# A new placement of the first 40 rounds of an attention and SoLU feed-forward kernel: DMA queues, rounds and engines of the weight pieces, loads of later batches, products with v, and the first steady pair

## The chip, the core and the metric

The kernel runs on one core of a Trainium2 chip. The core has five engines that run side by side, each in its own order: TensorE (PE; its weight loads are listed apart as PEld), VectorE (DVE), ScalarE (ACT), GpSimd (POOL) and SyncE (SP), which only issues DMA transfers here. ScalarE can issue DMAs too, and then the issue stands in ScalarE's own order of work. The metric is the device time of one execution in microseconds (us).

## The reference: thresholded attention, then a feed-forward layer with SoLU

All data are float32, except that the two weight matrices arrive as float64.

```python
# attention: q, k, v of shape (8, 8, 576, 64), tau = 0.02
scores = (1/8) * q @ k^T
scores = where(scores >= max(scores) - tau, scores, -1e9)
attn   = exp(scores - max) / (sum + 1e-9)
x      = (attn @ v), heads put side by side: (4608, 512)
# feed-forward: w_in (512, 1024), w_out (1024, 512), g_ln (1024)
h    = x @ w_in
solu = h * softmax(h)
ln   = (solu - mean) / sqrt(var + 1e-6) * g_ln
out  = ln @ w_out
```

## The kernel before

**Rounds.** The attention is cut into 144 rounds ("slots"), 18 for each of the 8 batches. A round takes 128 query rows of a pair of heads (or the left-over rows of four heads) against all 576 keys. Its steps are: scores on PE (`scores`, L492); the row's threshold on VectorE (`maxes`, L514); ramp and exponential on ScalarE (`ramp` L529, `exps` L538); one round later the sums' reciprocal and the scaling on GpSimd (`normalise`, L545 to L548) and the transposes of 32x32 blocks on VectorE (`blocks`, L559), which fill a tile T. After every second round DMAs on SP's queue move T into wT with its quarters of rows in place (`spread`, L580, L582, L589). Some rounds later PE multiplies wT with v (`attend_steps`, L619), and ScalarE copies the product to xh or xe (`attended`, L652).

**Feed-forward.** A group of 128 tokens gets h on PE (L1041 before round 30; L735 for pairs of groups and L759 for single groups after), then a chain of maximum, exponential, product, sums, mean and variance, and normalisation (L1056 to L1130), a transpose through DMAs (V, L1144) and VectorE (uT, L1157), the product with w_out on PE (L1175), a copy `ob` (L1195) and the store (L1216). Groups that are done before round 30 are called fronts; their steps stand in the table `HO` and `CHAIN`. From round `START` = 30 on, `steady_round` runs the same work in a fixed pattern: `new_pair` treats two groups together with the steps of `PAIR0` (first pairs), `PAIR` or `PAIRZ`, and `new_one` a single group by `ONE0`, `ONE` or `ONEZ`. In these tables a step has a place in a round (0 to 3: begin, early, middle, late) and a number of rounds after the group's start.

**Weights.** The weights are float64 and are turned into float32 by integer arithmetic in 16 pieces of 128x512 (pieces 0 to 7 of w_in, 8 to 15 of w_out). A piece has up to six jobs: `weight_load` (DMA into one of four raw buffers, chosen by `RAW`; the queue is ScalarE's where `QUEUE` is 1, else SP's), `weight_a` (one scaling `em` by the engine that `UNIT` names: 0 VectorE and 2 GpSimd at L286, 1 ScalarE at L282; the sign on VectorE, L291; the low half on ScalarE, L294), `weight_b` (VectorE, L306), `weight_c` (GpSimd, L316), `weight_gain` (the gain g_ln, by `GAIN`: 0 ScalarE L322, 1 VectorE and 2 GpSimd L324) and `weight_d` (copies of two halves to other rows, by `MOVER`: 0 ScalarE L337, 1 VectorE L339, 2 GpSimd L343, 3 DMA L347). `PIECE` gives the quarter of a round of each job (round = number // 4), `MOVE` that of the copies. Before round 0, pieces 0 to 2 are loaded. A raw buffer that is used again is loaded only when all three reads of `weight_a` of the piece before are done.

**Loads.** The q, k and v of batch 0 are loaded at the start and, for the later half of v, at the rounds in `FETCH`; batch 1's by `FETCH` as well. From batch 2 on q and k arrive as they lie in memory (`load_natural`) and are turned by VectorE ("flip", L209) and DMAs (L211). `LOAD2`, `TURN2`, `ENDS2` and `V2` say in which round batch 2's loads, turns, end rows and parts of v stand. `PREP` says in which rounds the k and q of batch 1 are turned on PE (L360) in the free part of the scores' PSUM tiles, and `EASED` whether ScalarE alone copies them out or shares this with VectorE (L396 to L439).

**Order.** Everything is recorded in the order of the program text, round by round, and each engine runs its instructions in that order. [...] `LAG` changes in which round after `LAG_PV` = 3 a product with v falls due, `SPLIT` how many of its matmuls run in the first of two rounds, and `SEVEN` when GpSimd forms sums of blocks of w_in (L692), which the pairs use.

```python
            jobs_of = zip(
                (2, 3, 1, 0, 4, 5),
                (weight_load, weight_a, weight_b, weight_c, weight_gain, copies),
                (*PIECE[x], MOVE.get(x, PIECE[x][4])),
            )
...
            pv_due.append((s + LAG_PV + LAG.get(s, 0), (b, kind, hp)))
```

Of the kernel before, what the change touches and what calls it, by code (L numbers as in the profile page):

```python
# [1582 lines left out]
```

## Time and profile before

| | |
|---|---|
| median of 3 runs | 845.41 us (841.01 to 851.94) |
| the profiled execution | 846.98 us |
| its span, first to last instruction | 845.0 us |
| granted TensorE clock, mean | 0.981 |
| PE busy | 799.7 us, 95% |
| VectorE, ScalarE, GpSimd busy | 671.5, 604.4, 565.2 us |
| DMA traffic | 167.44 MB, mean 198 GB/s |

A profile records one execution. A row of a group tells line, engine, operation, tile written <- tiles read, shape and count, then the busy time, the mean duration in ns, and the engine's idle time just before these instructions with what ended it. Slices are 1/40 of the span; a digit is the busy share in tenths. A row with "q" behind the engine's name (SPq, ACTq) belongs to its sequencer: an issue or a wait. The DMA share is the mean busy share of 16 DMA engines.

### The profile page before, as it was taken

To read this page: it belongs to the slowest core of one execution; us is meant where nothing else is said; L and a number is where in the kernel's file an instruction comes from. 1 tells how busy PE (TensorE), PEld (TensorE's weight loads), DVE (VectorE), ACT (ScalarE), POOL (GpSimd) and SP (SyncE) were. 2 spreads that over 40 slices of the span, in tenths; PEclk is the share of its full clock that TensorE was granted. 3 is DMA by queue.
4 is the path that set the end of the run, shared out by engine and by line. 5 is a ranking of instruction groups with operands and counts; after the bars stand their busy time and mean duration, and the time that the engine had idled before them with its cause. 6 is when DMAs were issued, how large, how long until landed. Compare 5 with 4: busy or idle time off the path is not lost.

```text
span 845.0 us, 36864 instructions
## 1 busy us (share of the span) xinstructions
PE 799.7 (95%) x15345; PEld 589.3 (70%) x15345; DVE 671.5 (79%) x1324; ACT 604.4 (72%) x1214; POOL 565.2 (67%) x1031
## 2 busy tenths in 40 slices
PE   4769899999899999999999999999999999999997
PEld 3435567767566886777776677767786677788786
DVE  3888968867889878888889888888888888787362
ACT  5979977676777777778787777878787687876231
POOL 3976867866757758585867758585867758574330
PEclk9679999999999999999999999999999999999999
DMA  7999688887877868887788768887788767555122
GB/s 231 272 231 259 181 221 225 213 220 191 222 224 208 228 149 240 229 216 207 204 244 223 204 163 246 225 221 196 216 238 218 207 159 211 144 152 137 37 62 52
DMA packets 100535, 167.44 MB, mean 198 GB/s; under 512 B 18248, under 2 KB 47952, under 8 KB 100368
## 3 DMA queue, kind: packets, MB, share of 16 engines
q1 hardware_dynamic: 99040, 162.82, 72.3%
q8 instruction: 121, 1.98, 1.0%
q10 hardware_dynamic: 1328, 2.26, 0.9%
q14 instruction: 46, 0.38, 0.1%
HBM read 46.14 MB, written 9.44 MB: 66 GB/s over the span
## 4 chain that ended last, share of the span: by engine, by line
PE 75%; ACT 7%; DMA 5%; POOL 4%; DVE 4%; issue 3%; SPq 2%; DVEq 0%; ACTq 0%; POOLq 0%
PE ov L1175 19%; PE h L735 16%; PE s_ps L492 14%; PE ov L619 12%; PE o_ps L1175 6%; PE h L759 4%; DMA wT<-T 3%; ACT w L529 2%; ACT w L538 2%; PE h_ps L1041 2%; DVE w L514 2%; PE pv L619 2%; POOL w L548 1%; DMA raw<-in_moe_w_out_dram 1%; DMA q<-in_q_dram 1%
## 5 line engine op out<-in xcount | busy, mean ns | idle before, releaser
L529 ACT ACTIVATE w<-s_ps,nth 128x576 f32<-128x576 f32 x282 | 199.6, 741 | 128.5 <-DVE nth L514 113.8
L514 DVE CUSTOM_DVE_ANT_0 w<-s_ps,tau_t 128x576 f32<-128x576 f32 x282 | 201.0, 749 | 55.0 <-PE s_ps L492 36.8
L548 POOL TENSOR_SCALAR w<-w,sm 128x576 f32<-128x576 f32 x288 | 219.0, 772 | 14.3
L559 DVE STREAM_TRANSPOSE T<-w 128x576 f32<-128x576 f32 x288 | 207.7, 756 | 17.8 <-POOL w L548 13.8
L538 ACT ACTIVATE w<-w,ntau 128x576 f32<-128x576 f32 x288 | 219.7, 768 | 0.0
L1175 PE MATMUL ov<-w,uT 64*64 64x256 f32 x3456 | 208.0, 376 | 0.7 <-issue 0.7
L492 PE MATMUL s_ps<-kT,qT 64*64 64x64 f32 (+1 forms) x2048 | 175.4, 424 | 15.1 <-ACT w L529 12.5
L619 PEld LDWEIGHTS ov<-wT,v 64*64 64x64 f32 x4752 | 150.6, 133 | 46.9 <-issue 33.6
L1175 PEld LDWEIGHTS ov<-w,uT 64*64 64x64 f32 x3456 | 160.6, 133 | 26.2 <-issue 1.2
L619 PE MATMUL ov<-wT,v 64*64 64x128 f32 (+1 forms) x4752 | 153.6, 259 | 1.2 <-DMA wT<-T 0.7
L545 POOL TENSOR_SCALAR sm<-sm 128x2 f32<-128x2 f32 x144 | 35.1, 244 | 143.5 <-ACT w L538 138.2
L546 POOL TENSOR_TENSOR sm<-sm,mone 128x2 f32<-128x2 f32 x144 | 104.1, 723 | 12.0
L735 PE MATMUL h<-w,xh 64*64 64x512 f32 x832 | 104.7, 591 | 0.6 <-POOL mark L110 0.4
L492 PEld LDWEIGHTS s_ps<-kT,qT 64*64 64x64 f32 x2048 | 71.4, 139 | 42.3 <-ACT w L529 19.1
L1175 PE MATMUL o_ps<-w,uT 64*64 64x256 f32 x1088 | 66.4, 377 | 0.7 <-ACT xh L652 0.5
L735 PEld LDWEIGHTS h<-w,xh 64*64 64x64 f32 x832 | 43.9, 133 | 31.4 <-issue 20.4
L1175 PEld LDWEIGHTS o_ps<-w,uT 64*64 64x64 f32 x1088 | 57.5, 133 | 10.8 <-issue 4.0
L1130 DVE TENSOR_SCALAR u<-u,rs,nb 128x1024 f32<-128x1024 f32 x32 | 28.8, 900 | 43.4 <-ACT V L1124 43.3
L1157 DVE STREAM_TRANSPOSE uT<-V 128x1024 f32<-128x1024 f32 x36 | 44.3, 1229 | 17.1 <-PE ov L1175 6.9
L538 ACT ACTIVATION_READ_ACCUMULATOR w<-w,ntau 128x1 f32 x288 | 55.7, 193 | 0.0
L735 PE MATMUL h<-k,sum 64*64 64x512 f32 x312 | 51.8, 589 | 0.0
L1124 ACT ACTIVATE V<-u,nb,rs 128x1024 f32<-128x1024 f32 x36 | 44.6, 1238 | 6.5 <-POOL nb L1102 6.4
(132 smaller groups left out, 1015.9 us busy)
## 6 DMA issues: line engine op xcount, KB each, us to landing
wT<-T SPq DMA_DIRECT2D x132, 288.0 KB, 4.5
wT<-T SPq DMA_DIRECT2D x256, 144.0 KB, 3.9
out_dram<-ob SPq DMA_DIRECT2D x71, 128.0 KB, 2.5
V<-u SPq DMA_DIRECT2D x136, 64.0 KB, 2.3
wT<-T SPq DMA_DIRECT2D x14, 576.0 KB, 6.4
q<-in_q_dram SPq DMA_DIRECT2D x24, 288.0 KB, 3.8
q<-in_k_dram SPq DMA_DIRECT2D x24, 288.0 KB, 4.3
v<-in_v_dram SPq DMA_DIRECT2D x12, 576.0 KB, 5.3
```

The lines of the kernel that those rows point to most:

```text
L492: nc.tensor.matmul(out=ps[h][ROWS[y], ks], lhsT=lhsT, rhs=d["kT"][ROWS[h], ks], start=True, stop=True,)
L514: nc.vector.tensor_tensor_reduce(out=w, in0=ps[:, 0:S], in1=(zero if loose else tau_t).to_broadcast([P, S]), scale=1.0, scalar=BIG, op0=AL ...
L529: nc.scalar.activation(out=d["w"][x], in_=d["w"][x] if d["loose"] else d["ps"][x][:, 0:S], func=AF.Prelu, bias=d["nth"][x], scale=-1.0, al ...
L538: nc.scalar.activation(out=w, in_=w, func=AF.Exp, bias=ntau, scale=1.0, accum_out=sm[:, x : x + 1])
L546: nc.gpsimd.tensor_tensor(out=sm, in0=sm, in1=mone, op=ALU.pow)
L548: nc.gpsimd.tensor_scalar(out=w, in0=w, scalar1=sm[:, x : x + 1], scalar2=1.0, op0=ALU.mult, op1=ALU.mult)
L559: nc.vector.transpose(out=T[:, :, r, :, h, :], in_=w.rearrange("p (c m x) -> p c m x", c=2, x=32))
L619: nc.tensor.matmul(out=to, lhsT=d["v"][ROWS[u], (h0 + h - u) % 4 if b > 1 else h0 + h, m ^ 4 * u if m < 8 and b < 2 else m,], rhs=rhs, sta ...
L735: mm = nc.tensor.matmul(out=h[ROWS[y], 512 * bank : 512 * bank + 512], lhsT=x[ROWS[r], ROWS[y]], rhs=w[ROWS[r]], start=c == 0 and (n, r, k ...
L1124: nc.scalar.activation(out=V, in_=u, func=AF.Identity, bias=nb, scale=rs)
L1157: nc.vector.transpose(out=uT, in_=d["V"].rearrange("p y (m x) -> p m y x", x=32))
L1175: nc.tensor.matmul(out=to[ROWS[z], 0:256], lhsT=d["uT"][ROWS[r], m].rearrange("p y x -> p (y x)"), rhs=w2[ROWS[r], m ^ r, 256 * z : 256 * ...
```

## The change

Only tables change, with no change to the arithmetic. Pieces 3 to 6 are issued from ScalarE's queue, and the quarters of rounds of the jobs of nearly all pieces are set anew. Scalings, gains and copies go to other engines. Loads, turns and parts of v of batches 1 and 2 get other rounds, the lags of three products with v become smaller, the splits move by a few matmuls, and the tables of the first single groups and the first pair get new places. In a table such as `CHAIN` the order of entries matters too where two steps fall on the same place.

```diff
     PAIR0 = {
+        "sum_b": (3, 8),
         "sums_a": (3, 0),
         "keep_a0": (3, 0),
-        "add_a0": (1, 1),
+        "norm_a": (3, 8),
         "sums_b": (2, 1),
+        "keep_b1": (3, 3),
+        "add_a1": (0, 5),
+        "max_a": (0, 5),
+        "add_b1": (0, 5),
+        "add_a0": (3, 0),
+        "exp_a": (1, 5),
         "keep_a1": (2, 3),
-        "keep_b1": (3, 3),
-        "add_a1": (3, 4),
-        "add_b1": (0, 5),
-        "max_a": (1, 5),
-        "exp_a": (1, 5),
+        "turn_a": (1, 10),
         "mul_a": (3, 6),
-        "sum_a": (0, 7),
+        "norm_b": (0, 12),
...
-        "stats_b": (0, 10),
+        "turn_b": (2, 14),
+        "stats_b": (3, 9),
+        "sum_a": (0, 7),
         "scale_b": (1, 11),
-        "norm2_b": (3, 12),
+        "norm2_b": (1, 13),
     }
     ONE0 = {
         "max": (0, 3),
+        "mul": (3, 3),
         "exp": (0, 3),
-        "mul": (1, 3),
-        "stats": (2, 4),
-        "sum": (1, 5),
+        "turn": (3, 9),
+        "stats": (3, 4),
         "scale": (3, 6),
-        "norm": (0, 7),
-        "norm2": (1, 7),
-        "turn": (3, 9),
+        "norm2": (0, 8),
+        "sum": (1, 4),
+        "norm": (3, 6),
     }
-    SPLIT = {30: 0, 32: 30, 34: 6, 36: 5, 38: 16, 40: 30, 42: 7, 44: 23, 46: 11, 56: 27, 74: 21, 92: 23, 110: 26, 128: 14}
-    SEVEN = {0: 21, 1: 21, 2: 24, 3: 25, 5: 25, 4: 26, 7: 26, 6: 29}
-    PIECE = {0: (-1, 1, 3, 6, 7, ), 1: (-1, 3, 5, 10, 11, ), 2: (-1, 8, 11, 14, 15, ), 3: (3, 12, 15, 18, 19, ), 4: (3, 15, 18, 21, 25, ), 5: (7, 20, 23, 26, 27, ), 6: (11, 23, 25, 30, 31, ), 7: (13, 27, 31, 34, 35, ), 8: (23, 31, 35, 38, 39, ), 9: (23, 35, 39, 42, 43, ), 10: (29, 39, 43, 46, 47, ), 11: (35, 43, 47, 50, 51, ), 12: (39, 49, 51, 54, 55, ), 13: (43, 52, 55, 58, 59, ), 14: (43, 55, 59, 62, 63, ), 15: (55, 59, 63, 66, 67, )}
+    SPLIT = {30: 0, 32: 32, 34: 0, 36: 4, 38: 14, 40: 34, 42: 8, 44: 20, 46: 12, 56: 26, 74: 20, 92: 25, 110: 29, 128: 10}
+    SEVEN = {0: 17, 1: 21, 2: 25, 3: 25, 5: 26, 4: 26, 7: 25, 6: 28}
+    PIECE = {0: (-1, 0, 3, 6, 7), 1: (-1, 3, 5, 10, 11), 2: (-1, 8, 11, 14, 15), 3: (7, 12, 15, 18, 19), 4: (3, 15, 17, 21, 25), 5: (7, 18, 23, 26, 27), 6: (11, 23, 25, 30, 31), 7: (18, 27, 31, 34, 35), 8: (19, 31, 35, 38, 38), 9: (22, 35, 39, 42, 43), 10: (27, 39, 42, 46, 47), 11: (35, 44, 46, 50, 51), 12: (39, 47, 51, 55, 55), 13: (43, 52, 55, 58, 59), 14: (43, 55, 59, 62, 64), 15: (55, 59, 63, 66, 67)}
-    QUEUE = {0: 1, 1: 1, 2: 1, 3: 0, 4: 0, 5: 0, 6: 0, 7: 0, ...}
-    UNIT = {0: 0, 1: 2, 2: 2, 3: 2, 4: 1, 5: 2, 6: 1, 7: 1, 8: 1, 9: 0, 10: 1, 11: 1, 12: 1, 13: 1, 14: 0, 15: 0}
-    GAIN = {8: 1, 9: 0, 10: 1, 11: 0, 12: 2, 13: 0, 14: 0, 15: 2}
-    MOVER = {16: 0, 17: 0, 18: 2, 19: 1, 20: 2, 21: 0, 22: 3, 23: 3, 24: 0, 25: 0, 26: 3, ...}
-    MOVE = {8: 47, 9: 55, 10: 55, 13: 63, 14: 70, 15: 67}
-    EASED = {0: 0, 1: 1, 2: 1, 3: 1, 4: 1, 5: 1, 6: 1, 7: 0, 8: 1, 9: 1, 10: 0, 11: 1, 12: 0, 13: 0, 14: 0, 15: 1, 16: 1, 17: 0, 18: 0, 19: 1, 20: 1, 21: 0}
+    QUEUE = {0: 1, 1: 1, 2: 1, 3: 1, 4: 1, 5: 1, 6: 1, 7: 0, ...}
+    UNIT = {0: 2, 1: 0, 2: 0, 3: 2, 4: 0, 5: 0, 6: 0, 7: 2, 8: 2, 9: 1, 10: 2, 11: 1, 12: 1, 13: 1, 14: 0, 15: 2}
+    GAIN = {8: 0, 9: 2, 10: 1, 11: 0, 12: 0, 13: 2, 14: 0, 15: 2}
+    MOVER = {16: 1, 17: 1, 18: 2, 19: 1, 20: 2, 21: 0, 22: 3, 23: 3, 24: 0, 25: 1, 26: 3, ...}
+    MOVE = {8: 46, 9: 58, 10: 57, 13: 68, 14: 69, 15: 70}
+    EASED = {0: 1, 1: 1, 2: 0, 3: 1, 4: 0, 5: 0, 6: 1, 7: 0, 8: 1, 9: 0, 10: 0, 11: 0, 12: 0, 13: 0, 14: 1, 15: 1, 16: 1, 17: 0, 18: 0, 19: 1, 20: 0, 21: 0}
-    PREP = {0: 14, 1: 14, 2: 14, 3: 15, 4: 15, 5: 17, 6: 16, 7: 16, 8: 19, 9: 19, 10: 18, 11: 20, 12: 20, 13: 22, 14: 21, 15: 21}
-    LAG = {1: 2, 3: 1, 5: 1, 9: 1, 11: 1, 17: 0, 21: 0, 23: 1, 25: 1}
-    FETCH = {0: 10, 1: 8, 2: 8, 3: 11, 4: 15, 5: 15, 6: 13, 7: 17, 8: 17, 9: 19, 10: 21, 11: 25, 12: 0, 13: 0, 14: 3, 15: 5}
-    LOAD2 = {0: 20, 1: 17, 2: 24, 3: 21, 4: 31, 5: 31, 6: 32, 7: 34}
-    TURN2 = {0: 23, 1: 24, 2: 27, 3: 28, 4: 33, 5: 34, 6: 36, 7: 37}
-    ENDS2 = {0: 30, 1: 28, 2: 42, 3: 44}
-    V2 = {0: 21, 1: 27, 2: 32, 3: 35}
+    PREP = {0: 14, 1: 14, 2: 14, 3: 15, 4: 17, 5: 15, 6: 15, 7: 16, 8: 19, 9: 21, 10: 20, 11: 20, 12: 19, 13: 21, 14: 21, 15: 21}
+    LAG = {1: 2, 3: 1, 5: 1, 9: 1, 11: 0, 17: -2, 21: 0, 23: -2, 25: 1}
+    FETCH = {0: 10, 1: 8, 2: 11, 3: 13, 4: 15, 5: 15, 6: 13, 7: 15, 8: 17, 9: 19, 10: 21, 11: 25, 12: 0, 13: 0, 14: 2, 15: 5}
+    LOAD2 = {0: 20, 1: 17, 2: 27, 3: 21, 4: 32, 5: 31, 6: 34, 7: 34}
+    TURN2 = {0: 23, 1: 24, 2: 31, 3: 25, 4: 35, 5: 34, 6: 36, 7: 38}
+    ENDS2 = {0: 32, 1: 34, 2: 49, 3: 44}
+    V2 = {0: 20, 1: 24, 2: 30, 3: 27}
```

In `CHAIN` the sums of three fronts stand earlier (entries 3: (1, 2) to (3, 1); 23: (3, 1) to (2, 1); 33: (1, 2) to (0, 2)), the copy out of the third front one place earlier (28: (2, 1) to (1, 1)), and the turn and copy out of the fourth later (37: (1, 6) to (2, 7); 38: (0, 1) to (2, 1)). `HO` differs in one entry that has no effect.

More of the change, by code (lines that the diff above doesn't have):

```diff
@@ L948 @@
-    UNIT = {0: 0, 1: 2, 2: 2, 3: 2, 4: 1, 5: 2, 6: 1, 7: 1, 8: 1, 9: 0, 10: 1, 11: 1, 12: 1, 13: 1, 14: 0, 15: 0}
-    GAIN = {8: 1, 9: 0, 10: 1, 11: 0, 12: 2, 13: 0, 14: 0, 15: 2}
-    MOVER = {16: 0, 17: 0, 18: 2, 19: 1, 20: 2, 21: 0, 22: 3, 23: 3, 24: 0, 25: 0, 26: 3, 27: 3, 28: 3, 29: 2, 30: 3, 31: 3}
-    MOVE = {8: 47, 9: 55, 10: 55, 13: 63, 14: 70, 15: 67}
-    EASED = {0: 0, 1: 1, 2: 1, 3: 1, 4: 1, 5: 1, 6: 1, 7: 0, 8: 1, 9: 1, 10: 0, 11: 1, 12: 0, 13: 0, 14: 0, 15: 1, 16: 1, 17: 0, 18: 0, 19: 1, 20: 1, 21: 0}
@@ L959 @@
-    ENDS2 = {0: 30, 1: 28, 2: 42, 3: 44}
-    V2 = {0: 21, 1: 27, 2: 32, 3: 35}
-    HO = {0: 11, 1: 12, 2: 17, 3: 18, 4: 13, 5: 14, 6: 22, 7: 23, 8: 20, 9: 21, 10: 26, 11: 27, 12: 24, 13: 25, 14: 32, 15: 32}
-    CHAIN = {0: (3, 0), 1: (3, 0), 2: (3, 1), 3: (1, 2), 4: (2, 2), 5: (0, 3), 6: (2, 3), 7: (3, 4), 8: (0, 1), 9: (3, 1), 10: (3, 2), 11: (3, 2), 12: (3, 3), 13: (3, 3), 14: (2, 4), 15: (0, 5), 16: (1, 6), 17: (3, 6), 18: (0, 1), 19: (0, 1), 20: (0, 1), 21: (0, 1), 22: (0, 2), 23: (3, 1), 24: (2, 2), 25: (3, 2), 26: (2, 3), 27: (3, 4), 28: (2, 1), 29: (3, 1), 30: (3, 0), 31: (3, 0), 32: (3, 1), 33: (1, 2), 34: (2, 2), 35: (2, 2), 36: (0, 4), 37: (1, 6), 38: (0, 1), 39: (2, 2)}
+    QUEUE = {0: 1, 1: 1, 2: 1, 3: 1, 4: 1, 5: 1, 6: 1, 7: 0, 8: 0, 9: 0, 10: 0, 11: 0, 12: 0, 13: 0, 14: 0, 15: 0}
@@ new lines @@
+    UNIT = {0: 2, 1: 0, 2: 0, 3: 2, 4: 0, 5: 0, 6: 0, 7: 2, 8: 2, 9: 1, 10: 2, 11: 1, 12: 1, 13: 1, 14: 0, 15: 2}
+    GAIN = {8: 0, 9: 2, 10: 1, 11: 0, 12: 0, 13: 2, 14: 0, 15: 2}
+    MOVER = {16: 1, 17: 1, 18: 2, 19: 1, 20: 2, 21: 0, 22: 3, 23: 3, 24: 0, 25: 1, 26: 3, 27: 3, 28: 3, 29: 2, 30: 3, 31: 3}
+    MOVE = {8: 46, 9: 58, 10: 57, 13: 68, 14: 69, 15: 70}
+    EASED = {0: 1, 1: 1, 2: 0, 3: 1, 4: 0, 5: 0, 6: 1, 7: 0, 8: 1, 9: 0, 10: 0, 11: 0, 12: 0, 13: 0, 14: 1, 15: 1, 16: 1, 17: 0, 18: 0, 19: 1, 20: 0, 21: 0}
```

8 lines of the change are left out of this document (2 added, 6 removed).

## The prediction

> **What bounds the kernel now.** I read the page's first two parts first, then the busy times by stage, then the start in detail.
>
> ```profile
> span 845.0 us, 36864 instructions
> PE 799.7 (95%) x15345; PEld 589.3 (70%) x15345; DVE 671.5 (79%) x1324; ACT 604.4 (72%) x1214; POOL 565.2 (67%) x1031
> ...
> PE   4769899999899999999999999999999999999997
> ...
> DMA  7999688887877868887788768887788767555122
> ```
>
> TensorE is the bound, but not in the left fifth of the span. The same by stages (the window, its length, then busy time of PE, PEld, DVE, ACT, POOL, the granted clock, the DMA share and GB/s):
>
> ```profile
> 12.00:66.00 54.00, 36.69 (x613) 22.98 (x605) 42.53 (x84) 44.14 (x99) 42.14 (x54) 0.75 0.98 245
> 66.00:95.00 29.00, 27.06 (x522) 19.03 (x520) 26.94 (x57) 27.44 (x55) 22.54 (x35) 1.00 0.84 225
> 95.00:130.00 35.00, 28.61 (x743) 19.82 (x740) 24.59 (x45) 25.90 (x63) 25.04 (x41) 1.00 0.82 209
> 130.00:180.00 50.00, 47.12 (x844) 36.00 (x838) 41.38 (x82) 36.77 (x75) 39.33 (x67) 0.97 0.85 219
> 180.00:230.00 50.00, 47.02 (x922) 33.00 (x918) 41.57 (x79) 35.85 (x73) 34.44 (x64) 1.00 0.82 214
> 230.00:760.00 530.00, 528.83 (x10226) 389.79 (x10222) 451.41 (x906) 401.42 (x795) 373.48 (x701) 1.00 0.76 207
> ```
>
> From 230 to 760 us PE idles 1.17 us of 530: whatever the first 40 rounds save or lose by 230 us is carried to the end one for one. What can be saved is PE's idle time before: 17.3 us (54.00 less 36.69) from 12 to 66, 1.9 from 66 to 95, 6.4 from 95 to 130, 2.9 and 3.0 in the last two. From 12 to 66 the DMA share is 0.98: there DMA is the bound, and PE waits for what it brings. In order of time (start, length, what; PE's idle time before in brackets):
>
> ```profile
> 59.04 0.69 PE L619 MATMUL pv<-wT,v 64*64 64x128 f32 x4 [3.64 <-issue]
> 60.18 3.89 PE L619 MATMUL pv<-wT,v 64*64 64x128 f32 x66 [0.45 <-DMA wT<-T]
> ```
>
> The third product with v (round 9) starts when its wT lands, and the scores of round 10 stand behind it on PE. The chain of waits says the same of this place:
>
> ```profile
> 39.40 9.06 DMA raw<-in_moe_w_out_dram
> ...
> 48.48 11.65 DMA wT<-T
> ```
>
> So two transfers in a row, 20.7 us, carry the chain: a full queue. But the queue was not always full. By 2 us (PE, clock, DMA share, GB/s), with SP's issues and SP's waits (total, times, longest):
>
> ```profile
> 16.00:18.00 2.00, 1.43 (x8) 1.00 0.28 111
> 18.00:20.00 2.00, 0.33 (x4) 1.00 0.34 63
> ...
> 13.01 5.55 SPq L267 DMA_DIRECT2D raw<-in_moe_w_in_dram  x2
> 18.61 1.74 SPq L174 DMA_DIRECT2D v<-in_v_dram  x3
> ...
> 25.07 0.62 SPq L580 DMA_DIRECT2D wT<-T  x1
> ...
> SPq L580 <- DVE T L559: 14.8, 5, 5.0
> SPq L267 <- ACT w L294: 4.2, 1, 4.2
> ```
>
> From 16 to 20 us DMA stands at 0.28 and 0.34. SP holds the load of weight piece 4, which waits 4.2 us until ScalarE (L294) has read piece 0 out of the same buffer, and the loads of v stand behind it.
>
> **The change part by part.** The sum is made against the profiled execution: span 845.0 and 1.98 around it, 846.98; the median of the runs, 845.41, is 1.57 lower.
>
> *Queues (QUEUE, PIECE).* Pieces 3 to 6 go from SP to ScalarE's queue. SP now issues v right after the last load of k and q, at about 13 us instead of 18.6; nothing that these loads wait for is late (v's buffer is new). Piece 4 is issued by ScalarE after the L294 that it waited for, in ScalarE's own order, so that wait is gone for everybody. Up to the wT of round 9 the set of transfers ahead is the same in both programs: q, k, v of the first batch, pieces 0 to 9, three wT. With the same work and DMA at about 1.0 elsewhere, the wall at 60.18 moves by the idle share that gets filled: 2.00 x (1 - 0.28) + 2.00 x (1 - 0.34) = 2.76 us. I take **-2.75**. Bounds: 0, if DMA idles later instead; -4.2, the whole of SP's wait. It is not more at the wall, whatever ScalarE saves, since DMA is the later of the two there.
>
> The price is on ScalarE, which now issues four loads in rounds 0 to 2. What an issue there can do is shown at the start:
>
> ```profile
> 8.65 0.33 ACTq L267 DMA_DIRECT2D raw<-in_moe_w_in_dram  x1
> 9.03 0.37 ACT L420 COPY kT<-tp 128x256 f32<-128x256 f32 x1 [4.38 <-DMA q<-in_q_dram]
> ...
> 17.45 1.30 ACT L294 ACTIVATE w<-raw 128x512 int32<-128x512 uint32 x2
> ...
> 21.34 0.75 ACT L294 ACTIVATE w<-raw 128x512 int32<-128x512 uint32 x1
> ...
> 26.52 0.72 ACT L294 ACTIVATE w<-raw 128x512 int32<-128x512 uint32 x1
> ...
> L267 ACTq DMA_DIRECT2D raw<-in_moe_w_in_dram x3: 334/335/599, 2.5 to 8.7; - x3
> ...
> DMA to landing us min/median/max: 4.9/9.1/10.2
> ```
>
> An issue waits until the DMA eight issues earlier has landed (completion semaphores are taken in turn), and the kT copy behind it idled 4.38 us for that. The new issues stand ahead of the L294 of rounds 0, 1 and 2, so ScalarE reaches them at about 17.4, 21.3 and 26.5 us. For piece 4 the earlier DMA is the k of pair 2, for 3 and 5 the k and q of pair 3, all through when DMA falls idle at 16 us. For piece 6 it is piece 4, issued 9.1 us before. Piece 4 needs 4.9 to 10.2 us by the row; with v nearly through by then I take 5, so no wait. The issues themselves, four of 0.33 to 0.60 us, delay ScalarE by at most 2.4 us, covered by PE's 4.1 us wait (3.64 + 0.45) at the wall; without that cover they cost 1.3 to 2.4. Every wT on SP keeps its place behind the same transfers.
>
> [...]
>
> *Engines (UNIT, GAIN, MOVER, EASED, PREP).* ScalarE, VectorE and GpSimd are near full from 66 to 95 us (27.4, 26.9 and 22.5 of 29). Prices (mean ns after the comma):
>
> ```profile
> L282 ACT ACTIVATE em<-raw 128x512 f32<-128x512 f32 x8 | 5.5, 683 | 0.0
> L337 ACT COPY w<-w 64x512 f32<-64x512 f32 x5 | 3.1, 617 | 0.1
> L322 ACT ACTIVATE w<-w,gs 128x512 f32<-128x512 f32 x4 | 3.0, 738 | 0.0
> ...
> L286 POOL TENSOR_SCALAR em<-raw 128x512 f32<-128x512 f32 x4 | 3.3, 821 | 11.0 <-DMA raw<-in_moe_w_in_dram 10.7
> L324 POOL TENSOR_SCALAR w<-w,gs 128x512 f32<-128x512 f32 x2 | 1.4, 692 | 0.2
> ...
> L286 DVE TENSOR_SCALAR em<-raw 128x512 f32<-128x512 f32 x4 | 1.7, 422 | 0.0
> L339 DVE TENSOR_SCALAR w<-w 64x512 f32<-64x512 f32 x1 | 0.4, 422 | 0.0
> ```
>
> Over the program ScalarE loses four L282 and three L337 (4.6 us); VectorE gains two L286 and three L339 (2.1 us) and loses one L324 and a few copies of k; GpSimd gains two L286 and one L324 (2.3 us). Rounds 3 to 9 lie before the DMA wall and count nothing. In rounds 10 to 14 I count, by the order of each engine: ScalarE one L322 and three L337 fewer (2.6), three small copies of k more, which I take at 0.36 us, between nothing and L337's 0.617, so -1.5; GpSimd one L286 more, +0.8; VectorE level. Which of the two ends last changes from round to round, so between -1.5 and +0.8 (+1.5 if the L324 that enters round 9 counts) I take **-0.5**.
>
> *Second and third batch (FETCH, LOAD2, TURN2, ENDS2, V2, SEVEN).* One place is visible. PE waits at 170.48 for the copy of ob, and the chain before it runs through VectorE:
>
> ```profile
> 164.28 0.73 DVE L209 STREAM_TRANSPOSE flip<-q 128x576 f32<-128x576 f32 x1
> 164.94 0.72 DVE L514 CUSTOM_DVE_ANT_0 w<-s_ps,zero 128x576 f32<-128x576 f32 x1
> ...
> 170.48 3.21 PE L619 MATMUL pv<-wT,v 64*64 64x128 f32 x72 [2.88 <-ACT ob L1195]
> ```
>
> Both flips of rounds 27 and 28 go elsewhere (to rounds 25 and 31, where PE is fuller). The first stands right before the maxima that end in ob: **-0.7**; -1.4 if both count, 0 if another wait comes up. The other loads move where SP has room; I cost them at nothing, covered by the rounds between load and use, and a load late by its landing would cost up to 4 us as the wait for the wT (3.64) did.
>
> *Products with v and the first pairs (LAG, SPLIT, PAIR0, ONE0, CHAIN).* PE's order stays but for turns of k and q in rounds 14 to 21 and some products of 2 to 6 matmuls split otherwise: the shorter lags find no free round. Steps of the first pair move by a phase or two. PE idles 3.0 us from 180 to 230; between -3.0 and, for one uT come late (1.2 us by L1157's mean on the page), +1.2, I take **0**, the row of 230 to 760 being next to it.
>
> ```profile
> L1157 DVE STREAM_TRANSPOSE uT<-V 128x1024 f32<-128x1024 f32 x36 | 44.3, 1229 | 17.1 <-PE ov L1175 6.9
> ```
>
> Sum: 846.98 - 2.75 - 0.5 - 0.7 = 843.0, by the median 843.0 - 1.57 = **841.5 us**.
>
> **The rivals.**
> *The gap is only moved.* At 25.07 SP waits for T of rounds 0 and 1, as it does five times (14.8 us). If v and piece 4 are through before ScalarE issues pieces 3 and 5, DMA idles from 21 us on instead. For: ScalarE is full there, so its issues come late. Against: v and piece 4 are 1.7 MB, at the 245 GB/s of this stage 6.9 us from 16 on, and pieces 3 and 5 come at 21.3. Then 1.2 us are left: 844.2. [...]
> *More is freed.* Of PE's 8.3 us idle from 66 to 130, half goes because the front's sums now stand ahead of weight work on GpSimd and ScalarE is lighter. For: by the rows of 66 to 130 us PE waits while no engine is quite full. Against: GpSimd's total there grows. 4.1 us more: 837.4.
> *Slower: ScalarE stands behind its own issues.* Place: rounds 0 to 2. Price: 4.38 us a wait, as at 9.03. One wait and the issues, 4.4 + 2.4 = 6.8 us, still about fit under the wall's 4.1 us and the 2.0 that three fewer L282 give in rounds 3 to 8. It decides from 6.1 us lost there; two waits make 11.2, 5.1 too many, and the DMA lead is of no use: 846.98 - 1.2 + 5.1 = 850.9, by the median 849.3. For: pieces land up to 10.2 us after issue, against 9.1 us until piece 6. Against: that was with a full queue.
>
> **How the numbers follow.** Forecast 0.46, the gap only moved 0.22, more freed 0.17, slower 0.15. What a measurement can tell from no change is about 2%, 17 us; no case reaches it, since all of PE's idle time from 66 to 230 is 14.2 us. Faster by over 2%: 0.03, for a sum of all upper ends; slower: 0.02, for three waits on ScalarE. Within: 0.95. The runs before lie 11 us apart, so the range goes a little past the outer cases: 833 to 850.
>
> **What would show it.** DMA share above 0.8 from 16 to 20 us, v issued at about 13 us, and the third product with v starting near 57.4 instead of 60.18 prove the first term. ScalarE idle over 1 us behind one of its four issues proves the slower rival. PE idle at the wait for ob below 2.3 us proves the flips. The first maxima of round 30 start here:
>
> ```profile
> 175.45 0.76 DVE L514 CUSTOM_DVE_ANT_0 w<-s_ps,tau_t 128x576 f32<-128x576 f32 x1 [2.00 <-PE s_ps L492]
> ```
>
> At 171.5 they would show the whole sum. I am wrong if the rounds from 10 to 20 change by more than 2 us, for there I only weigh two engines against each other.

## The result and the profile after

The changed kernel takes 852.89 us (median; 848.53 to 859.08), the kernel before 848.09 in the same comparison: ratio 1.0070, interval 1.0044 to 1.0096. It is slower, by 0.7%, where 841.5 us and a small gain had been forecast. The 11.4 us between 841.5 and 852.89 are three parts: the kernel before is 2.7 us slower than its three runs had it (848.09 for 845.41), the forecast gain of 3.95 us is not there, and the change costs 4.8 us.

The profiled execution of the changed kernel has a span of 851.6 us, 6.6 more than that of before. From the first two parts of its page:

```profile
span 851.6 us, 36858 instructions
PE 800.5 (94%) x15345; PEld 578.7 (68%) x15345; DVE 672.8 (79%) x1327; ACT 600.5 (71%) x1208; POOL 567.3 (67%) x1034
...
PE   4578889999899999999999999999999999999997
...
DMA  9899788897777678876888758887788767555122
```

The work is the same; of the 6.6 us PE is busy for 0.8 and idle for the rest. The stages, with the columns as in the prediction (window, length, busy time of PE, PEld, DVE, ACT and POOL, granted clock, DMA share, GB/s):

```profile
230.00:760.00 530.00, 525.84 (x10128) 379.13 (x10124) 448.18 (x901) 399.54 (x791) 369.59 (x693) 1.00 0.76 206
12.00:66.00 54.00, 36.43 (x625) 24.45 (x617) 44.70 (x89) 43.40 (x97) 42.52 (x54) 0.81 0.94 249
66.00:95.00 29.00, 27.77 (x488) 19.97 (x492) 25.98 (x50) 24.18 (x52) 22.38 (x35) 0.94 0.82 214
95.00:130.00 35.00, 28.91 (x776) 20.59 (x772) 24.05 (x47) 25.70 (x61) 27.63 (x44) 1.00 0.81 209
130.00:180.00 50.00, 46.01 (x836) 34.15 (x832) 41.32 (x82) 36.76 (x76) 37.69 (x63) 1.00 0.86 221
180.00:230.00 50.00, 45.98 (x914) 32.02 (x908) 42.14 (x80) 34.77 (x71) 34.15 (x64) 0.97 0.79 212
```

From 12 to 66 us the DMA share fell from 0.98 to 0.94, where the prediction had a gap in the copies filled (GB/s hardly moved, 249 for 245). PE lost 1.1 and 1.0 us of work in the last two rows, and from 230 to 760 us, where the prediction had it idle for 1.17 us, it idles 4.16.

**First loss: a new gap in the copies.** The gap at 16 to 20 us is filled, as forecast, but another one stands at 36 to 40. After, then before:

```profile
16.00:20.00 4.00, 2.46 (x20) 0.59 (x12) 2.17 (x6) 4.00 (x12) 3.14 (x5) 1.00 1.08 266
36.00:40.00 4.00, 0.00 (x0) 0.00 (x0) 4.00 (x7) 2.09 (x7) 3.34 (x5) 0.91 0.09 34
```

```profile
36.00:40.00 4.00, 1.74 (x16) 1.14 (x20) 1.63 (x5) 4.00 (x12) 3.73 (x6) 0.80 1.02 298
```

What the copies wait for is on SP and, before it, on VectorE (DVE). SP and then DVE in time order after the change:

```profile
38.85 0.58 SPq L580 DMA_DIRECT2D wT<-T  x1
```

```profile
33.09 0.68 DVE L306 SCALAR_TENSOR_TENSOR em<-em 128x512 int32<-128x512 int32 x1
35.66 1.47 DVE L286 TENSOR_SCALAR em<-raw 128x512 f32<-128x512 f32 x1 [1.88 <-POOL w L316]
37.05 0.43 DVE L291 TENSOR_SCALAR em<-raw 128x512 int32<-128x512 int32 x1
37.40 1.42 DVE L559 STREAM_TRANSPOSE T<-w 128x576 f32<-128x576 f32 x2
38.75 0.71 DVE L514 CUSTOM_DVE_ANT_0 w<-s_ps,tau_t 128x576 f32<-128x576 f32 x1
```

and the same stretch of the kernel before, SP and DVE:

```profile
34.91 0.58 SPq L580 DMA_DIRECT2D wT<-T  x1
```

```profile
32.77 0.69 DVE L306 SCALAR_TENSOR_TENSOR em<-em 128x512 int32<-128x512 int32 x1
33.37 1.51 DVE L559 STREAM_TRANSPOSE T<-w 128x576 f32<-128x576 f32 x2
34.81 0.80 DVE L291 TENSOR_SCALAR em<-raw 128x512 int32<-128x512 int32 x1
35.52 0.74 DVE L514 CUSTOM_DVE_ANT_0 w<-s_ps,tau_t 128x576 f32<-128x576 f32 x1
```

The widening of piece 5 (weight_a, L286 and L291) has moved from GpSimd (POOL) to DVE (UNIT[5] from 2 to 0) and from quarter 20 to quarter 18 (PIECE). There it stands ahead of the transposition that makes T. Its output buffer is that of piece 3, which POOL's L316 still reads, so DVE stands 1.88 us, then works 1.9 us on the piece, and T, the copies of wT and the maxima of round 5 come 3 to 4 us later.

These two profiles do not show that the loss reaches the end: at round 10 the changed kernel is 1.95 us ahead of the profile of before (first maxima at 64.00 and 65.95), and at round 38 still 1.73. What round 5 costs has to come from the experiments.

**Second loss: the keys of round 40.** PE around 224 us after, and in the kernel before:

```profile
219.87 1.46 PE L619 MATMUL ov<-wT,v 64*64 64x64 f32 x88
224.18 2.20 PE L492 MATMUL s_ps<-kT,qT 64*64 64x64 f32 x16 [2.85 <-ACT w L538]
```

```profile
222.43 0.33 PE L492 MATMUL s_ps<-kT,qT 64*64 64x64 f32 x4 [0.63 <-ACT w L529]
223.11 1.19 PE L492 MATMUL s_ps<-kT,qT 64*64 64x64 f32 x12 [0.35 <-ACT w L529]
```

The row names ScalarE's L538, because that ended last. But before, the scores needed only L529. SP's issues, after and before:

```profile
214.65 3.56 SPq L1144 DMA_DIRECT2D V<-u  x4
218.30 0.63 SPq L580 DMA_DIRECT2D wT<-T  x1
218.97 1.25 SPq L582 DMA_DIRECT2D wT<-T  x2
220.32 1.20 SPq L211 DMA_DIRECT2D kT<-flip  x2
```

```profile
213.19 2.47 SPq L1144 DMA_DIRECT2D V<-u  x4
215.76 1.78 SPq L211 DMA_DIRECT2D kT<-flip  x2
```

TURN2[7], the round in which the last quarter of batch 2's keys is flipped, went from 37 to 38, so the copies of the flipped keys are issued 4.6 us later, behind three copies of wT. In the trace they land at 224.04 and 224.42, and the scores start at 224.18, just behind the first of them. So the keys are the suspects. From round 38 to round 43 the changed kernel loses 3.9 us (first maxima at 214.50 and 243.77 against 216.23 and 241.61).

**Third: PE idle in the steady part,** 3.0 us more. It waits for wT, for instance in round 92:

```profile
504.92 1.50 PE L619 MATMUL ov<-wT,v 64*64 64x64 f32 x72
507.04 0.33 PE L619 MATMUL ov<-wT,v 64*64 64x64 f32 x4 [0.62 <-DMA wT<-T]
508.05 0.58 PE L619 MATMUL ov<-wT,v 64*64 64x64 f32 x24 [0.67 <-DMA wT<-T]
```

Here SPLIT asks for 100 of the 144 matmuls before the next scores (92 before); from the 73rd on they need the second half of wT. Whether that is the cause is for the experiments.

### The profile page after: what moved, and what is told of

It reads as the page before. It is cut to its first block, busy times and chain, and to the rows that moved or that the text cites. A ratio compares the mean times of both kernels' runs of the same rounds, so it can differ in the third digit from the quotient of the medians.

```text
span 851.6 us, 36858 instructions
## 1 busy us (share of the span) xinstructions
PE 800.5 (94%) x15345; PEld 578.7 (68%) x15345; DVE 672.8 (79%) x1327; ACT 600.5 (71%) x1208; POOL 567.3 (67%) x1034
## 4 chain that ended last, share of the span: by engine, by line
PE 69%; DMA 7%; ACT 7%; POOL 6%; DVE 5%; SPq 3%; issue 3%; ACTq 0%; DVEq 0%; POOLq 0%
PE ov L1175 17%; PE h L735 14%; PE s_ps L492 13%; PE ov L619 11%; PE o_ps L1175 6%; DMA wT<-T 5%; PE h L759 4%; ACT w L529 2%; ACT w L538 2%; POOL w L548 2%; PE h_ps L1041 2%; DVE w L514 2%; PE pv L619 1%; DVE T L559 1%; POOL sm L546 1%
## 5 line engine op out<-in xcount | busy, mean ns | idle before, releaser
L529 ACT ACTIVATE w<-s_ps,nth 128x576 f32<-128x576 f32 x282 | 199.6, 740 | 137.3 <-DVE nth L514 123.7
L514 DVE CUSTOM_DVE_ANT_0 w<-s_ps,tau_t 128x576 f32<-128x576 f32 x282 | 201.1, 749 | 54.7 <-PE s_ps L492 36.2
L538 ACT ACTIVATE w<-w,ntau 128x576 f32<-128x576 f32 x288 | 219.6, 767 | 0.0
L619 PEld LDWEIGHTS ov<-wT,v 64*64 64x64 f32 x4752 | 148.3, 133 | 51.8 <-issue 39.6
L1175 PEld LDWEIGHTS ov<-w,uT 64*64 64x64 f32 x3456 | 155.5, 133 | 30.1 <-issue 0.8
L538 ACT ACTIVATION_READ_ACCUMULATOR w<-w,ntau 128x1 f32 x288 | 55.5, 193 | 0.0
```

What stands on the lines that cost most here:

```text
L514: nc.vector.tensor_tensor_reduce(out=w, in0=ps[:, 0:S], in1=(zero if loose else tau_t).to_broadcast([P, S]), scale=1.0, scalar=BIG, op0=AL ...
L529: nc.scalar.activation(out=d["w"][x], in_=d["w"][x] if d["loose"] else d["ps"][x][:, 0:S], func=AF.Prelu, bias=d["nth"][x], scale=-1.0, al ...
L538: nc.scalar.activation(out=w, in_=w, func=AF.Exp, bias=ntau, scale=1.0, accum_out=sm[:, x : x + 1])
L619: nc.tensor.matmul(out=to, lhsT=d["v"][ROWS[u], (h0 + h - u) % 4 if b > 1 else h0 + h, m ^ 4 * u if m < 8 and b < 2 else m,], rhs=rhs, sta ...
L1175: nc.tensor.matmul(out=to[ROWS[z], 0:256], lhsT=d["uT"][ROWS[r], m].rearrange("p y x -> p (y x)"), rhs=w2[ROWS[r], m ^ r, 256 * z : 256 * ...
```

## The experiments

Ratios are to the kernel before, run on the same chip, with 95% intervals. "Round 10" and the like is the start of that round's first maximum (DVE, L514) in the profiled execution.

**One part of the change undone.** Piece 5 back on POOL, its quarter left:

```diff
-UNIT[5] = 0
+UNIT[5] = 2
```

> The changed kernel with one entry of UNIT back: the widening of piece 5 (L286) on POOL, not DVE. Theory (DVE stood behind a full buffer): in the changed kernel DVE waited 1.88 us at 35.66 for POOL's L316 before that L286, then ran it in 1.47 us, with round 5's first maximum (38.75) and the transposition of T behind it. Without it the first maximum of round 5 starts near 35.6, SP's first wT issue of that round near 35.3 (38.85), the DMA share of 36 to 40 us goes from 0.09 to above 0.8, and round 10's first maximum comes 2 to 3.5 us earlier than 64.00. Device time, if all that is kept: 850 to 851 (the changed kernel had 852.9, the kernel before 848.1). Rival (the gap is the DMA queues' own, behind the weight loads that moved to ACT's queue): the gap stays, round 10 stays at 64.0, time 852 to 854. Second rival (early gains are eaten before round 38): the gap closes, round 38 is no earlier than 214.0, time 852 to 853.

Measured: 1.0027 (1.0000 to 1.0053), median 853.06. Round 5 at 37.77, DMA share at 36 to 40 us 0.29, round 10 at 62.14. The wait for POOL is gone, but the other half of the widening, L291, now stands ahead of T (35.10, 1.40 us). Half a cure: the first reading named only one of the two instructions. Both undone:

```diff
-UNIT[5] = 0;  PIECE[5] = (7, 18, 23, 26, 27)
+UNIT[5] = 2;  PIECE[5] = (7, 20, 23, 26, 27)
```

> The changed kernel with piece 5 widened where the kernel before does it: on POOL and from quarter 20, not on DVE from quarter 18. In the run with POOL alone DVE still ran L291 (35.10, 1.40 us) ahead of the transposition of T, and round 5 began at 37.77. Theory (piece 5 stands in front of T on DVE): round 5's first maximum at 35.5 to 36.3, the DMA share of 36 to 40 us above 0.6 (0.09 in the changed kernel), round 10's at 61 to 62.5. What it brings at the end: by the theory that rounds 13 to 16 are set by the copies, nothing: round 16 at 99 to 100.5, time 851.5 to 853.5; by the rival (one for one to the end), 2 to 3 us: 850 to 851.

Measured: 1.0024 (0.9992 to 1.0055), median 849.86. Round 5 at 36.27, DMA share 0.82 at 36 to 40 us, round 10 at 61.11, round 16 at 98.22. The gap is closed, and by the ratio (1.0070 to 1.0024) about 0.46% of the time goes with it. Of the 2.9 us won by round 10, 1.7 are left at round 16 (99.90 in the changed kernel), so the theory that all of it would be eaten up there was wrong. But a difference of two such ratios is itself uncertain by about 0.4%, an estimate from the half-widths of the two intervals (0.26 and 0.31%).

```diff
-TURN2[7] = 38
+TURN2[7] = 37
```

> The changed kernel with one entry of TURN2 back: quarter 7 is flipped in round 37 and not 38. Theory (keys late): in the changed kernel the two kT copies of that flip were issued at 220.32 and 220.92, behind three wT copies of SP, landed at 224.04 and 224.42, and PE stood 2.85 us at 224.18 before the scores of round 40. With round 37 they are issued 3 to 4 us earlier, the 2.85 us shrink below 0.8, round 41's first maximum comes 2 to 3 us earlier than 233.24, and the time falls by 2 to 2.8 us from 852.9 to 850 to 851. Rival (PE waits for ACT's exponentials, L538, as the row names it): the wait stays at 2 to 3 us, time 852 to 854.

Measured: 1.0028 (1.0000 to 1.0056), median 851.2. Rounds 38 to 43 lose 0.9 us instead of 3.9. PE ahead of round 40:

```profile
222.62 0.33 PE L492 MATMUL s_ps<-kT,qT 64*64 64x64 f32 x4 [0.72 <-ACT w L529]
223.30 1.19 PE L492 MATMUL s_ps<-kT,qT 64*64 64x64 f32 x12 [0.35 <-ACT w L529]
```

The wait is as short as before, and the scores wait for L529 again. It was the keys. In every profile of a kernel with 38 here PE stands 2.1 to 3.4 us, in every one with 37 it stands 0.6 to 0.7, then 0.35. In five of the six with 38 the trace has the landing of the first key copy, and the scores start 0.13 to 0.14 us behind it each time; three of these rows name the copy itself (kT<-flip) and not ScalarE.

```diff
-SPLIT[56, 74, 92, 110, 128] = 26, 20, 25, 29, 10
+SPLIT[56, 74, 92, 110, 128] = 27, 21, 23, 26, 14
```

> The changed kernel with the five SPLIT entries from round 56 on (26, 20, 25, 29, 10) as before (27, 21, 23, 26, 14). Theory (larger shares reach for copies that have not landed): in the changed kernel PE waited for wT at 507.04 and 508.05 (0.62 and 0.67) in round 92 and 1.37 at 641.84 in round 118, and from round 44 to 143 it lost 3.7 us against the kernel before. Those waits shrink below 0.3 in all, the loss from round 44 to 143 goes below 1, time 849 to 850.5. Rival (chance of when SP's single long issues of 1 to 2 us fall): waits of the same kind stay, at these or other rounds, and the time stays at 852 to 854.

Measured: 1.0041 (1.0014 to 1.0068), median 853.55; PE idles 4.44 us from 230 to 760 us, as much as with the new shares. The mirror, these five entries of the changed kernel in the kernel before:

> The kernel before with the five SPLIT entries from round 56 on as in the changed kernel (26, 20, 25, 29, 10). Theory (larger shares reach for copies that have not landed): waits of PE for wT in rounds 92 and 118 appear, 1 to 4 us in all, time 849.5 to 852, ratio 1.002 to 1.005. Rival (chance of SP's long issues): the same as before, 848 with a ratio within 0.999 to 1.001.

Measured: 0.9987 (0.9966 to 1.0009), median 849.37; PE idles 3.78 us from 230 to 760 us. So nothing speaks for these SPLIT entries as the cause, and the rival, chance, is left. It is taken up with the first steady pair below. The 1.0041 also shows how far one ratio can lie from the 1.0070 when nothing that matters is undone, so the two single cures above (1.0024 and 1.0028) do not prove a size by themselves.

**Parts alone, in the kernel before.** The queues:

```diff
-QUEUE[3..6] = 0;  PIECE[3] = (3, 12, 15, 18, 19)
+QUEUE[3..6] = 1;  PIECE[3] = (7, 12, 15, 18, 19)
```

> The kernel before with QUEUE 1 for pieces 3 to 6 and the load of piece 3 at quarter 7, and nothing else: the first term of the prediction alone. Theory of the prediction (the wall moves and what is won stays): DMA share of 16 to 20 us from 0.31 to above 0.8, round 10's first maximum near 63.2 (65.95 before), round 30's near 172.7 (175.45), time 2.75 us under the kernel before, ratio 0.9968. New theory (the gap in the copies only moves, and rounds 13 to 15 wait for what the copies still owe): a stretch of 4 us with a share under 0.6 appears between 24 and 44 us or 64 and 72 us, round 16's first maximum stays within 99.0 to 100.5 (99.83), ratio 0.998 to 1.002. Third (ACT stands behind its own four issues): ACT idles more than 1 us behind an issue, round 10 no earlier than 65.5, ratio 1.001 or more.

Measured: 1.0000 (0.9973 to 1.0028). The gap is filled:

```profile
16.00:20.00 4.00, 1.31 (x16) 0.65 (x16) 3.68 (x8) 3.59 (x9) 3.81 (x5) 1.00 1.18 215
```

Round 10 comes at 60.05, 5.9 us earlier than in the profile of before, and round 44 is still 6.5 us ahead. By this one profile the gain is double the forecast and stays; by the time there is none that the interval shows. No theory had both. The profile alone says little: kernels with the start of before have round 10 between 59.98 and 65.95 (see below), and 60.05 lies within that. ScalarE did not stand behind its issues (0.4 us at the most).

All tables of the first batch (QUEUE, PIECE, UNIT, GAIN, MOVER, MOVE, EASED, PREP, LAG, FETCH, SEVEN, HO, CHAIN), then those behind it (LOAD2, TURN2, ENDS2, V2, PAIR0, ONE0, SPLIT), each set alone:

```diff
-the set as in the kernel before
+the set as in the changed kernel
```

> The kernel before with the changed tables of the first batch alone (QUEUE, PIECE, UNIT, GAIN, MOVER, MOVE, EASED, PREP, LAG, FETCH, SEVEN, HO, CHAIN); loads and flips of the second batch, first steady pair and SPLIT as before. Theory (the loss of rounds 38 to 43, 3.9 us in the changed kernel's profile, sits in the other tables): round 43's first maximum stands to that of the kernel before as round 38's does, within 0.7 us, and the time is 0 to 2.5 us under the kernel before, ratio 0.997 to 1.000. Rival (the first batch's tables cost it): ratio 1.004 to 1.007, as the whole change has 1.007.

> The kernel before with the changed tables of the second batch and behind alone (LOAD2, TURN2, ENDS2, V2, PAIR0, ONE0, SPLIT); the mirror of the run with the first batch's tables. Theory (the loss of rounds 38 to 43 sits here): rounds 38 to 43 lose 2.5 to 4 us against the kernel before, PE stands 2 to 3 us ahead of round 40's scores, ratio 1.003 to 1.006. Rival (the first batch's tables cost it): ratio 0.999 to 1.001.

Measured: 1.0047 (1.0018 to 1.0076) and 1.0024 (0.9993 to 1.0054). The first half costs; for the second the interval includes 1. The expectation that all of it sat in the second half was wrong. With the late tables PE stands 2.55 us ahead of round 40 and rounds 38 to 43 lose 2.2; with the first batch's tables they lose 1.25, where 0.7 at the most was expected.

The engines, then the queues with the rounds of the pieces, piece 5 at quarter 20:

```diff
-UNIT, GAIN, MOVER, EASED, PREP as in the kernel before
+UNIT, GAIN, MOVER, EASED, PREP as in the changed kernel
```

> The kernel before with UNIT, GAIN, MOVER, EASED and PREP of the changed kernel and nothing else: the second term of the prediction alone. Theory of the prediction: rounds 10 to 14 get shorter by 0.5 us (bounds -1.5 and +1.5), ratio 0.9994. New theory (work taken from ScalarE lands on VectorE in front of the maxima of rounds 12 and 14): from round 10 to round 16 it loses 1.5 to 3.5 us (the changed kernel and its four variants lost 1.7 to 4.0 there; the kernels with the old front between a gain of 0.6 and a loss of 1.1), and L339 stands on DVE ahead of round 12's maximum; ratio 1.001 to 1.004. If the loss comes from the order of the pieces instead, rounds 10 to 16 stay within 0.7 of the kernel before.

```diff
-QUEUE[3..6], PIECE, MOVE as in the kernel before
+QUEUE[3..6], PIECE, MOVE as in the changed kernel;  PIECE[5] = (7, 20, 23, 26, 27)
```

> The kernel before with the queues, the rounds of the pieces (PIECE, MOVE) of the changed kernel, except piece 5, which is widened from quarter 20; engines as before. Theory (engines cost it, not the rounds of the pieces): rounds 10 to 16 within 1 us of the kernel before, no gap in the copies below a share of 0.5 between 32 and 44 us, ratio 0.996 to 1.000. Rival (the rounds of the pieces cost it): rounds 10 to 16 lose 1.5 to 3.5 us, ratio 1.001 to 1.004.

Measured: 0.9983 (0.9951 to 1.0016) and 0.9994 (0.9967 to 1.0020). From round 10 to 16 they lose 1.2 and 1.1 us, less than 1.5. So neither the engines nor the order of the other pieces costs anything that can be measured, and the theory that VectorE's new work in rounds 12 to 14 costs 1.5 to 3.5 us falls. Of the first batch's 0.47% piece 5 at quarter 18 is left, and LAG, FETCH, SEVEN, HO and CHAIN, which no run set alone.

The engines' run also parts two things that the change had put together. Piece 5's L286 is on DVE there too, but at quarter 20, and so behind the transposition:

```profile
32.87 1.42 DVE L559 STREAM_TRANSPOSE T<-w 128x576 f32<-128x576 f32 x2
34.23 1.37 DVE L286 TENSOR_SCALAR em<-raw 128x512 f32<-128x512 f32 x1
35.52 0.43 DVE L291 TENSOR_SCALAR em<-raw 128x512 int32<-128x512 int32 x1
```

Nothing waits for POOL, round 5 starts at 35.88, and the DMA share at 36 to 40 us is 1.05. So it is not the engine that makes the gap but the place: ahead of the transposition.

The first steady pair, twice:

```diff
-PAIR0, ONE0, SPLIT[30..46] as in the kernel before
+PAIR0, ONE0, SPLIT[30..46] as in the changed kernel
```

> The kernel before with PAIR0, ONE0 and the SPLIT entries of rounds 30 to 46 of the changed kernel: the last term of the prediction alone. Theory of the prediction: 0, ratio 1.000. New theory (L781 of the first pair now stands ahead of round 39's maximum on VectorE and waits for ScalarE's L774): round 39 is 0.7 to 1.4 us longer to the kernel before, rounds 38 to 43 lose 0.7 to 1.5 in all; ratio 1.000 to 1.002.

> Once more the kernel before with the first pair's tables and SPLIT of rounds 30 to 46 of the changed kernel, which had 0.9956 (0.9929 to 0.9983). Theory (the new order of the first pair wins about 2 us by itself): 0.994 to 0.998 again. Rival (chance: its profile showed the loss at round 39 and the gain at round 40 to cancel, and won at round 10, where its program is the one of the kernel before): 0.999 to 1.001.

Measured: 0.9956 (0.9929 to 0.9983), then 1.0019 (0.9988 to 1.0051). The interval of the first excludes 1, and the repetition did not bear it out. Round 39 did not get 0.7 to 1.4 us longer: in both profiles it is 0.76 shorter, and rounds 38 to 43 still lose 0.65 and 0.50. The two profiles of this one program differ by 5.2 us of span (840.7 and 845.9). The first has round 10 at 59.98, the second at 63.02; their steady parts, one row of each:

```profile
230.00:760.00 530.00, 528.29 (x10220) 384.44 (x10215) 451.01 (x903) 403.23 (x800) 374.14 (x701) 1.00 0.76 205
```

```profile
230.00:760.00 530.00, 525.71 (x10142) 389.88 (x10138) 450.04 (x901) 398.95 (x792) 371.56 (x696) 1.00 0.75 205
```

PE idles 1.71 us in the one and 4.29 in the other. That is the "third loss" without any change of the program. Over all profiles of this study this idle time lies between 1.0 and 7 us; the profile of before, with 1.17, was near the lucky end, while its start (round 10 at 65.95) was the latest of all.

**The two spots together.** Undone in the changed kernel, and alone in the kernel before:

```diff
-UNIT[5] = 0;  PIECE[5] = (7, 18, 23, 26, 27);  TURN2[7] = 38
+UNIT[5] = 2;  PIECE[5] = (7, 20, 23, 26, 27);  TURN2[7] = 37
```

> The changed kernel with both spots as before: piece 5 widened on POOL from quarter 20, quarter 7 flipped in round 37. Theory (these two carry the loss): from the ratios measured one by one, 1.0070 less 0.0046 (1.0070 to 1.0024 by piece 5) less 0.0042 (1.0070 to 1.0028 by quarter 7) = 0.998; 0.995 to 1.001. PE's wait ahead of round 40 below 0.8, round 5's first maximum at 36 to 36.5. Rival (they overlap, or a third place carries as much): 1.002 to 1.004.

```diff
-UNIT[5] = 2;  PIECE[4][2] = 18;  PIECE[5][1] = 20;  TURN2[7] = 37
+UNIT[5] = 0;  PIECE[4][2] = 17;  PIECE[5][1] = 18;  TURN2[7] = 38
```

> The kernel before with these two spots alone: piece 5 widened on DVE from quarter 18 (and piece 4's L306 at 17, which has to be ahead of it), quarter 7 flipped in round 38. Theory (these two carry the loss): ratio 1.005 to 1.009; PE's wait ahead of round 40 2.5 to 3.4 us, round 5's first maximum at 37.5 to 39, a DMA share below 0.5 at 36 to 40 us. Rival (they cost only beside the rest of the change): 0.999 to 1.003.

Measured: undone 0.9999 (0.9974 to 1.0024), median 849.46; alone 1.0036 (1.0003 to 1.0069), median 851.05, less than the 1.005 to 1.009 expected, with a wait of 2.13 us ahead of round 40 for an expected 2.5 to 3.4. The same DVE stretch undone:

```profile
33.56 1.06 DVE L306 SCALAR_TENSOR_TENSOR em<-em 128x512 int32<-128x512 int32 x1
34.55 1.43 DVE L559 STREAM_TRANSPOSE T<-w 128x576 f32<-128x576 f32 x2
35.90 0.38 DVE L291 TENSOR_SCALAR em<-raw 128x512 int32<-128x512 int32 x1
36.20 0.74 DVE L514 CUSTOM_DVE_ANT_0 w<-s_ps,tau_t 128x576 f32<-128x576 f32 x1
```

and with the two spots alone, DVE and PE:

```profile
35.69 1.47 DVE L286 TENSOR_SCALAR em<-raw 128x512 f32<-128x512 f32 x1 [1.80 <-POOL w L316]
37.09 0.43 DVE L291 TENSOR_SCALAR em<-raw 128x512 int32<-128x512 int32 x1
37.44 1.42 DVE L559 STREAM_TRANSPOSE T<-w 128x576 f32<-128x576 f32 x2
```

```profile
226.70 1.49 PE L492 MATMUL s_ps<-kT,qT 64*64 64x64 f32 x16 [2.13 <-ACT w L538]
```

Without the two spots the loss is gone, and the kernel before with nothing but them has the same waits in the same places and is slower, if only by an interval that just excludes 1. Their size is less sure: 0.71% by undoing them, 0.36% by adding them, and the intervals overlap. That round 5 costs time further on is seen over many profiles. Among the kernels with the new queues, round 30 starts between 174.31 and 176.66 in the four with piece 5 on DVE at quarter 18, and between 170.03 and 173.90 in the eight with it on POOL at quarter 20 (the half cure, on POOL at quarter 18, has 174.38).

**What is left of the change.** Queues and second loads; then, on top of these, all other parts that did not cost, run twice; then the same without the first pair:

```diff
-QUEUE[3..6], PIECE[3][0], LOAD2, TURN2, ENDS2, V2 as in the kernel before
+the same as in the changed kernel, but TURN2[7] = 37
```

> The kernel before with the queues (pieces 3 to 6 on ScalarE's, piece 3 from quarter 7) and the loads of the second batch (LOAD2, TURN2, ENDS2, V2) of the changed kernel, except quarter 7's flip, which stays in round 37; engines, pieces, first pair and SPLIT as before. Theory (these are the parts that win): rounds 25 to 38 take 1.5 to 2.6 us less than in the kernel before, PE's wait ahead of round 40 is below 0.8, rounds 38 to 43 within 0.7 of it; ratio 0.994 to 0.998, 844 to 848 us. Rival (the queue's win is chance of one run, the loads win nothing): ratio 0.998 to 1.001.

```diff
-UNIT, GAIN, MOVER, EASED, PREP, PAIR0, ONE0, SPLIT[30..46] as in the kernel before
+the same as in the changed kernel, but UNIT[5] = 2
```

> The kernel before with all parts that did not cost by themselves: queues, engines (piece 5 on POOL), loads of the second batch with quarter 7 in round 37, first pair and SPLIT to round 46; the rounds of the pieces as before. Theory (the parts add up): 0.9956 (first pair) with 0.9983 (engines), 1.0000 (queues), 0.9986 (queues and loads) makes 0.992 to 0.996, 842 to 846 us. Rival (single ratios below 1 are chance, or the parts stand in each other's way): 0.998 to 1.002.

> Once more the kernel of the parts that did not cost by themselves (0.9951, 0.9917 to 0.9984). Theory (the parts win together): 0.993 to 0.998 again, 845 to 848 us. Rival (chance, as with the first pair alone): 0.999 to 1.002.

> The same kernel with the first pair's tables and SPLIT as before. Theory (the first pair's order brings nothing by itself, 0.9956 and 1.0019): the same ratio as its neighbour within 0.3%, 0.993 to 0.999. Rival (it wins only where the keys of round 40 come in time): 0.998 to 1.002.

Measured: 0.9986 (0.9956 to 1.0017) for queues and loads; 0.9951 (0.9917 to 0.9984) and, repeated, 0.9992 (0.9962 to 1.0023) for all parts; 1.0001 (0.9972 to 1.0030) without the first pair. The expected 1.5 to 2.6 us in rounds 25 to 38 were 0.6 with queues and loads. The kernel of all parts is about 1% faster than the changed kernel (the mean of its two ratios, 0.997, to 1.007). That it beats the kernel before is not shown: the repetition did not bear it out.

## Why the prediction was wrong

The forecast was 846.98 - 3.95 - 1.57 = 841.5; 852.89 was measured.

**The base: 2.7 us too low.** The median of the three runs shown, 845.41, became 848.09 with more of them, and the profiled execution, 846.98, was quicker than the new median, not 1.57 slower as the sum had it. The working took the span's places for fixed. The wall at 60.18 was not: kernels with exactly this start have their round 10 at 65.95, 65.91, 61.78, 59.98 and 63.02, and the profile of before is the latest of them. In the quickest, the third product:

```profile
54.73 4.21 PE L619 MATMUL pv<-wT,v 64*64 64x128 f32 x70
```

**"The wall moves by the idle share that gets filled": -2.75.** That the gap is filled, and that v goes out early, was right (shares of 1.08 and 1.18 for 0.31). In time the queues alone brought 0 (interval -2.3 to +2.4 us), so the term is too large, at the least by its excess over 2.3. The 66 matmuls of the third product, forecast for 57.4, began at 59.01 in the changed kernel.

**"Every wT on SP keeps its place behind the same transfers": false.** Its place in SP's order stayed; the T that it waits for did not. This is the step that failed first. It goes back to "VectorE gains two L286 ... Rounds 3 to 9 lie before the DMA wall and count nothing": one of these L286 is piece 5's. It made T, and with it SP's first copy of that round, 3.9 us later (38.85 for 34.91). Before this wall of copies an engine does not count only as long as it issues no copy and feeds none; DVE feeds every wT. The rival of a gap that is only moved (0.22) had the right form; it put the gap at 21 us and ScalarE's issues as the reason, and it gave 844.2 and not a loss.

**Engines, -0.5:** alone 0.9983 (0.9951 to 1.0016). The term is 0.06% of the time, so this run can neither confirm it nor rule it out.

**Second loads, -0.7 and nothing else.** The wait for ob went from 2.88 to 2.62 us: -0.26, short of the 2.3 that was named as its proof. The step that failed is "the other loads move where SP has room; I cost them at nothing". The bound named there, up to 4 us for something that lands late, was right: PE stood 2.85 us where it had stood 0.98 in two parts (0.63 and 0.35), for a flip moved by one round. SP's order of issues at this place, which is fixed before any run, shows the key copies behind three wT; it was not looked at, because the cover was reckoned in rounds.

**Products with v and first pair, 0:** not contradicted by 0.9956 and 1.0019 for the first pair; the new lags were not run alone.

**"Whatever the first 40 rounds save or lose is carried to the end one for one":** what piece 5 costs in round 5 is still there at round 30 (above), and 0.71% of the time is gone at the end when both spots are undone. But the steady part adds between 1 and 7 us of its own to a profiled execution, more than any term of the sum.

**The slower rival,** ScalarE behind its own issues, did not come: in no profile with the new queues does it idle for more than 1.0 us behind one of the four. The wait that gave its price is in the trace of before: ScalarE's issue at 8.65 came 0.02 us behind the landing of the q that SP issued at 2.02, eight issues ahead of it. The loss has another mechanism than the one that carried the chance for it.

**The sign for the whole sum:** round 30 at 171.5 for 175.45. In the changed kernel it came at 174.68, 0.8 us earlier and not 3.95.

## What to carry to other kernels

When work is moved to an engine that executes in order, look for what stands behind its first wait, and whether that feeds a copy: here one instruction that waited 1.9 us for a buffer and ran 1.5, with its second half of 0.4 behind it, held up a full DMA queue by 3.9 us, and the same instruction placed behind the transposition held up nothing. Count the cover of a moved load in issues of its queue, not in rounds. And where the steps argued over are 0.1 to 0.5% of the span, one profile is one draw, and even an interval that excludes 1 wants a repetition when it is the best of many.
